# One PSUM bank tag: where the hash products stand while attention runs beside layer 1

## The chip, the core and the metric

The program runs on one core of one Trainium2 chip. TensorE (PE) multiplies into PSUM, which holds eight banks of 2 KB on each of 128 partitions; VectorE (DVE), ScalarE (ACT) and GpSimd (POOL) do the rest, and SyncE (SP) issues most DMAs. Each engine works through its own instructions in order and waits on semaphores for the others. The metric is the time of one execution in microseconds of device time; lower is better.

## What is computed

Two batches of eight heads of hashed attention feed two gated layers. Cut to what matters:

```python
q_bits = (einsum('bhsd,dk->bhsk', q, proj) > 0)      # 6 hash bits of each query, k_bits alike
mask   = q_bucket[:, :, :, None] == k_bucket[:, :, None, :]
scores = where(mask, scale * q @ k.T, -1e9)
attn   = softmax(scores);  x = attn @ v               # x: 1536 tokens x 512
g      = x @ w_gate                                   # layer 1, d_ff 1536
x      = (g * sigmoid(g) * (x @ w_val)) @ w_out
h      = x @ w_in                                     # layer 2, d_ff 2048
out    = (max(h, 0) + alpha * min(h, 0)) @ w_out2
```

## The kernel before

**Stages.** Tokens go in three chunks of 512. First the attention of chunk 0 runs alone. Then layer 1 of chunk 0 and of chunk 1 (`stage1`) run with the attention of the next chunk woven between their matrix products, two steps of attention to each step of layer 1 at most (`RATES`); this is the stretch "beside layer 1". After it come layer 1 of chunk 2 and layer 2 of all chunks, without attention.

**Attention.** An item is one pair of heads and 256 queries; it has two units, one for each head. A unit passes four parts, each a slot later than the one before (`LAGS`): `banks` (three score tiles `S` of two products each, copied out by ACT into `se`, their maxima `m` formed by DVE), `top` (the maxima transposed on PE into `mt`, reduced by DVE into `mq`), `back` (`mq` spread by PE into `mb`, subtracted by DVE at L341, exponent on ACT) and `values` (products with V into `po`, normalised by DVE as `xf` at L380).

**Hash products.** Preparing an item takes the hash of its queries, and each new pair of heads takes the hash of its keys in two pieces. `hash_mm` (L200 to L208) multiplies into a tile `hp` on PE; `hash_bits` (L212) reads it on DVE into the bits `mk`, and with that the bank is free; `hash_rows` (L218) copies `mk` into the operands of the scores on ACT. `mk` has one buffer. Beside layer 1 there are 21 such products: 8 for keys, all in the first third, and 13 for queries.

**Banks.** All PSUM tiles come from one pool, by tag: `at.nb` gives S three banks, T one, G two, Y one, po one. A tile of a tag must wait until the readers of the tile that last stood in its bank are done. Beside layer 1 the score tiles and `hp` take turns in the three banks of S, `mt` stands in Y, `mb` in T, the products of layer 1 (`gp`) in the two banks of G, and `po` in its own. The table is a line of its own:

```python
at.nb = dict(S=3, T=1, G=2, Y=1, po=1)
at.tag = dict(mt="G", mb="G", hp="T", po=("Y", "po"), gates="G")     # attention alone
at.tag = dict(mt="Y", mb="T", hp="S", po=("po", "po"), gates="G")    # beside layer 1
```

**Order.** The program text gives the order of the steps, and a scheduler then sets each engine's order from it, from the waits between the tiles and its own estimate of times; a few instructions are pinned. Weights come in as 64-bit words by DMA (`raw`, two buffers shared with the keys), are rounded by ACT (L596), DVE (L597, L599) and POOL (L601) into `wt`, split by ACT (L636) and DVE or POOL (L643) into `wb`, and the halves go to `gp` on PE at L699 to L701.

Of the kernel before, what the change touches and what calls it, by code (L numbers as in the profile page):

```python
# [54 lines left out]
def lsh_attention_moe_kernel(  # L55
# [13 lines left out]
    B, H, D, S = qT.shape  # L69
# [65 lines left out]
    at = Bag()  # L135
# [487 lines left out]
    def w_early():  # L623

        for w in early:
            r = raw_load(w)
            yield
            t = wp.tile([P, 512], F32, tag="wt", name="wt", bufs=WB[0])
            round64(r, t.bitcast(I32))
            yield  # L630
            nc.sync.dma_start(out=whole[w - F2I], in_=t)
            yield
# [231 lines left out]
        k += 1  # L864
        prime(k)
    at.alone = False
    at.tag = dict(mt="Y", mb="T", hp="S", po=("po", "po"), gates="G")
    early_steps = w_early()
    ws.pin = False
    ws.busy = True  # L870
# [98 lines left out]
```

## Time and profile before

| | |
|---|---|
| median of 3 runs | 845.91 us (845.59 to 846.26) |
| the profiled execution | 843.88 us |
| its span, first to last instruction | 842.0 us |
| beside layer 1 | about 118 to 445 us of the span |
| PE busy | 813.0 us, 97% |
| DVE, ACT, POOL busy | 536.6, 442.7, 347.5 us |

Three views are read. The windows give each engine's busy time and PE's granted clock in a stretch. The waits name who waited for whom. The timeline lists instructions: start, duration, engine, line, operation, what it writes and reads, and in square brackets the idle time of the engine just before it and what ended that. A product of PE overlaps the next one, so the distance between two starts (0.23 us for `gp`, 0.12 us for S) says more than a duration.

### The profile page before, as it was taken

To read this page: it belongs to the slowest core of one execution; us is meant where nothing else is said; L and a number is where in the kernel's file an instruction comes from. 1 tells how busy PE (TensorE), PEld (TensorE's weight loads), DVE (VectorE), ACT (ScalarE), POOL (GpSimd) and SP (SyncE) were. 2 spreads that over 40 slices of the span, in tenths; PEclk is the share of its full clock that TensorE was granted. 3 is DMA by queue.
4 is the path that set the end of the run, shared out by engine and by line. 5 is a ranking of instruction groups with operands and counts; after the bars stand their busy time and mean duration, and the time that the engine had idled before them with its cause. 6 is when DMAs were issued, how large, how long until landed. Compare 5 with 4: busy or idle time off the path is not lost.

```text
span 842.0 us, 11156 instructions
## 1 busy us (share of the span) xinstructions
PE 813.0 (97%) x3988; PEld 681.7 (81%) x3988; DVE 536.6 (64%) x826; ACT 442.7 (53%) x738; POOL 347.5 (41%) x284
## 2 busy tenths in 40 slices
PE   5998899998999999999999999999999999999998
PEld 4777778887888888888888888887888888888886
DVE  5889998887898866656675342348986533334332
ACT  7889877877766645555544232224433333333331
POOL 5133337666755633222221352333543354445441
PEclk9999999999999999999999999999999999999999
DMA  9223346867656547554554787784300300010001
GB/s 246 69 69 98 128 120 203 253 220 241 219 202 234 174 152 260 199 179 149 175 188 141 249 286 235 262 282 170 138 1 0 151 1 0 1 51 1 0 1 51
DMA packets 57287, 122.03 MB, mean 145 GB/s; under 512 B 16912, under 2 KB 29200, under 8 KB 56720
## 3 DMA queue, kind: packets, MB, share of 16 engines
q1 hardware_dynamic: 56080, 118.51, 42.3%
q0 software_dynamic: 1008, 2.75, 1.6%
q8 instruction: 32, 0.52, 0.3%
q14 instruction: 23, 0.19, 0.1%
q10 hardware_dynamic: 144, 0.05, 0.0%
HBM read 94.03 MB, written 27.26 MB: 144 GB/s over the span
## 4 chain that ended last, share of the span: by engine, by line
PE 70%; DVE 9%; DMA 7%; ACT 7%; issue 4%; POOL 1%; SPq 0%; DVEq 0%; ACTq 0%; POOLq 0%
PE po L358 9%; PE gp L699 8%; PE gp L701 8%; PE gp L700 8%; PE op L705 5%; PE op L706 5%; PE op L704 5%; DMA raw<-in_wblk_dram 5%; PE hp L700 5%; PE hp L699 5%; PE hp L701 5%; PE S L304 2%; PE S L305 2%; ACT se L306 2%; DVE wt L599 1%
## 5 line engine op out<-in xcount | busy, mean ns | idle before, releaser
L694 POOL TENSOR_TENSOR gl<-ex,gh 128x512 fp32r<-128x512 f32 x81 | 110.2, 1360 | 191.8 <-ACT gh L691 174.5
L358 PE MATMUL po<-se,vv 128*128 128x256 f32 x576 | 139.2, 381 | 5.4 <-ACT se L347 2.8
L691 ACT ACTIVATE gh<-ex 128x512 fp32r<-128x512 f32 x84 | 53.0, 631 | 137.1 <-DVE ex L688 86.6
L358 PEld LDWEIGHTS po<-se,vv 128*128 128x128 f32 x576 | 106.2, 190 | 22.7 <-ACT se L347 4.6
L699 PE MATMUL gp<-xh,wb 128*128 128x512 f32 x288 | 120.1, 417 | 0.5 <-ACT xh L383 0.5
L701 PE MATMUL gp<-xh,wb 128*128 128x512 f32 x288 | 112.9, 392 | 0.0
L700 PE MATMUL gp<-xl,wb 128*128 128x512 f32 x288 | 112.7, 391 | 0.0
L636 ACT ACTIVATE wb<-w 128x512 fp32r<-128x512 f32 x96 | 59.7, 628 | 71.4 <-PE hp L701 57.6
L601 POOL TENSOR_TENSOR wt<-wt,wr 128x512 int32<-128x512 int32 x48 | 63.4, 1327 | 81.1 <-DVE wt L599 32.8
L685 DVE TENSOR_SCALAR ex<-hp,al 128x512 f32<-128x512 f32 x48 | 35.9, 748 | 93.2 <-PE hp L701 92.0
L306 ACT ACTIVATE se<-S 128x512 f32<-128x512 f32 x144 | 81.9, 593 | 23.7 <-PE S L305 22.7
L304 PE MATMUL S<-QA,kt 128*128 128x256 f32 x288 | 79.6, 303 | 6.8 <-ACT se L306 3.0
L341 DVE SCALAR_TENSOR_TENSOR se<-se,mb 128x1536 f32<-128x1536 f32 x48 | 83.5, 1740 | 3.4 <-PE mb L336 3.4
L347 ACT ACTIVATE se<-se 128x1536 f32<-128x1536 f32 x48 | 71.1, 1482 | 8.8 <-DVE se L341 8.6
L705 PE MATMUL op<-wb,gh 128*128 128x512 f32 x192 | 74.8, 390 | 0.9 <-DVE wb L643 0.9
L305 PE MATMUL S<-qb,kt 76*128 76x256 f32 x288 | 73.9, 286 | 1.0 <-ACT kt L218 0.6
L706 PE MATMUL op<-wb,gl 128*128 128x512 f32 x192 | 74.7, 389 | 0.0
L699 PE MATMUL hp<-xh,wb 128*128 128x512 f32 x192 | 74.7, 389 | 0.0
L700 PE MATMUL hp<-xl,wb 128*128 128x512 f32 x192 | 74.7, 389 | 0.0
L701 PE MATMUL hp<-xh,wb 128*128 128x512 f32 x192 | 74.7, 389 | 0.0
L704 PE MATMUL op<-wb,gh 128*128 128x512 f32 x192 | 74.7, 389 | 0.0
L643 DVE TENSOR_TENSOR wb<-w,wb 128x512 fp32r<-128x512 f32 x65 | 56.1, 866 | 17.4 <-ACT wb L636 17.4
(99 smaller groups left out, 1666.7 us busy)
## 6 DMA issues: line engine op xcount, KB each, us to landing
wb<-w SPq DMA_DIRECT2D x72, 512.0 KB, 4.1
raw<-in_wblk_dram SPq DMA_DIRECT2D x68, 512.0 KB, 4.6
w<-wb SPq DMA_DIRECT2D x36, 512.0 KB, 3.0
qr<-in_q_dram SPq DMA_DIRECT2D x24, 256.0 KB, 2.9
nat<-in_k_dram SPq DMA_DIRECT2D x8, 384.0 KB, 3.4
vv<-in_v_dram SPq DMA_DIRECT2D x16, 192.0 KB, 5.6
whole<-wt SPq DMA_DIRECT2D x12, 256.0 KB, 2.2
w<-whole SPq DMA_DIRECT2D x12, 256.0 KB, 4.3
```

The lines of the kernel that those rows point to most:

```text
L304: nc.tensor.matmul(pt[:, i, :], lhsT=ka[:, sl], rhs=qa, start=True, stop=False)
L305: nc.tensor.matmul(pt[:, i, :], lhsT=kb[:, sl], rhs=qb, start=False, stop=True)
L306: nc.scalar.activation(out=u.se[:, 2 * j:2 * j + 2, :], in_=pt, func=AF.Copy)
L341: ins = nc.vector.scalar_tensor_tensor(out=u.se, in0=u.se, scalar=FLOOR, in1=u.mx[:, None, :].to_broadcast([P, NC, GQ]), op0=ALU.max, op1= ...
L358: nc.tensor.matmul(it.po[:, u.x, :], lhsT=VV[it.b, it.p][:, kb, u.x * D:u.x * D + P], rhs=u.se[:, kb, :], start=kb == 0, stop=kb == NC - 1)
L694: eng.tensor_tensor(out=l, in0=ex, in1=f32(h), op=ALU.subtract)
L699: nc.tensor.matmul(pt, lhsT=h, rhs=ah, start=first, stop=False)
L700: nc.tensor.matmul(pt, lhsT=h, rhs=al_, start=False, stop=False)
L701: nc.tensor.matmul(pt, lhsT=l, rhs=ah, start=False, stop=last)
L704: nc.tensor.matmul(pt, lhsT=gh, rhs=h, start=first, stop=False)
L705: nc.tensor.matmul(pt, lhsT=gh, rhs=l, start=False, stop=False)
L706: nc.tensor.matmul(pt, lhsT=gl, rhs=h, start=False, stop=last)
```

## The change

One tag: beside layer 1 `hp` now asks for the bank of tag Y, in which only `mt` stood, and no longer for one of the three of tag S. Sizes, counts and arithmetic stay.

```diff
-    at.tag = dict(mt="Y", mb="T", hp="S", po=("po", "po"), gates="G")
+    at.tag = dict(mt="Y", mb="T", hp="Y", po=("po", "po"), gates="G")
```

With other banks the scheduler finds other waits and sets some instructions elsewhere. In the rows below a name ends in the number of its tile, so that the two orders can be told apart; `waits` names the engines whose semaphores the instruction waits on.

PE, around the second piece of the keys' hash of the second new pair (hp_1808) and the next transposes; the order is the same on both sides, and the waits are not:

```order
 L206 MATMUL hp_1808<-kt1_125,skh_62 44x384
 L207 MATMUL hp_1808<-kt1_125,skl_63 44x384
-L304 MATMUL S_1813<-QA_1347,kt3_127 128x256 [waits Activation_49]
+L304 MATMUL S_1813<-QA_1347,kt3_127 128x256
 L305 MATMUL S_1813<-qb1_67,kt3_127 128x256
 L304 MATMUL S_1813<-QA_1347,kt3_127 128x256
...
 L330 MATMUL mt_1843<-ident_71,m2_1692 128x128 [waits DVE_49]
...
-L358 MATMUL po_1875<-se_1410,vv_386 128x256 [waits DVE_49,Activation_49]
+L358 MATMUL po_1875<-se_1410,vv_386 128x256 [waits PE_49,Activation_49]
 L358 MATMUL po_1875<-se_1410,vv_386 128x256
```

The score tile behind hp_1808 waits for nobody now; mt_1843 still waits on DVE, in the changed kernel for the reader of hp_1808 as well; and the po behind it no longer needs a wait on DVE of its own.

PE, around the second piece of the keys' hash of the third new pair (hp_2077), whose transposes are mt_2083:

```order
 L206 MATMUL hp_2077<-kt2_126,skh_62 44x384
 L207 MATMUL hp_2077<-kt2_126,skl_63 44x384
-L330 MATMUL mt_2083<-ident_71,m2_1957 128x128 x2
 L699 MATMUL gp_2062<-gh_1622,wb_1990 128x512
 L700 MATMUL gp_2062<-gl_1623,wb_1990 128x512
...
 L699 MATMUL gp_2062<-gh_1733,wb_1990 128x512
 L700 MATMUL gp_2062<-gl_1734,wb_1990 128x512
+L330 MATMUL mt_2083<-ident_71,m2_1957 128x128 x2
 L701 MATMUL gp_2062<-gh_1733,wb_1990 128x512
 L336 MATMUL mb_2100<-ident_71,mq_1963 128x128 x2
```

The transposes now stand behind five products of layer 1. Behind four of the hashes of queries the transposes move behind three products in the same way.

ACT, a little later, where the weights raw_2236 are rounded:

```order
 L596 ACTIVATE wr<-raw_2170 128x512
-L676 ACTIVATE ex<-gp 128x512
-L306 ACTIVATE se<-S 128x512
-L347 ACTIVATE se<-se 128x1536
-L306 ACTIVATE se<-S 128x512
-L636 ACTIVATE wb<-wt 128x512
-L306 ACTIVATE se<-S 128x512
-L218 ACTIVATE qb_66<-mk 12x256 x2
 L596 ACTIVATE wr<-raw_2236 128x512
```

The rounding of raw_2236 stands ahead of a tanh, three copies of scores and an exponent now, and no longer behind them; on DVE L597 and L599 for raw_2236 likewise stand ahead of a bit test L212, and SP issues that load two places earlier.

## Rows read from the trace of the kernel before

**Rows 1.** The page, part 1: busy time, share of the span, instructions.

```profile
PE 813.0 (97%) x3988; PEld 681.7 (81%) x3988; DVE 536.6 (64%) x826; ACT 442.7 (53%) x738; POOL 347.5 (41%) x284
```

**Rows 2.** Windows: stretch, length, busy PE, PEld, DVE, ACT, POOL, granted clock, DMA.

```profile
118.00:445.00 327.00, 321.55 (x1666) 273.72 (x1665) 249.15 (x400) 207.93 (x351) 151.35 (x119) 0.99 0.60 200
```

**Rows 3.** Waits of PE, 118 to 445 us: who for whom, total, times, longest.

```profile
PE po L358 <- DVE xf L380: 2.2, 3, 0.9
PE S L304 <- DVE mk L212: 1.7, 2, 1.4
PE hp L206 <- ACT se L306: 0.9, 1, 0.9
```

**Rows 4.** Timeline, PE and DVE, the first hash of keys beside layer 1.

```profile
136.76 0.53 PE L206 MATMUL hp<-kt,skh 128*44 128x384 f32 x1
...
137.38 0.41 DVE L331 TENSOR_REDUCE mq<-mt 128x2 f32<-128x256 f32 x1
```

**Rows 5.** Timeline, PE, a score tile that waits for a bit test.

```profile
155.56 0.28 PE L305 MATMUL S<-qb,kt 76*128 76x256 f32 x1
156.16 0.38 PE L304 MATMUL S<-QA,kt 128*128 128x256 f32 x1 [0.32 <-DVE mk L212]
```

**Rows 6.** Timeline, PE, the transposes mt_1843 and the po behind them.

```profile
169.55 0.38 PE L330 MATMUL mt<-ident,m 128*128 128x128 f32 x2
...
172.06 1.10 PE L358 MATMUL po<-se,vv 128*128 128x256 f32 x4 [0.53 <-DVE xf L380]
```

**Rows 7.** Timeline, DVE, the same time, and a later L179 for comparison.

```profile
165.68 2.49 DVE L179 TENSOR_TENSOR kt<-nat,kt 64x768 fp32r<-64x768 f32 x1
168.20 1.68 DVE L599 SCALAR_TENSOR_TENSOR wt<-raw,wt 128x512 int32<-128x512 int32 x1
172.55 0.60 DVE L212 TENSOR_SCALAR mk<-hp,ck 44x384 f32<-44x384 f32 x1
...
193.09 0.95 DVE L179 TENSOR_TENSOR kt<-nat,kt 64x768 fp32r<-64x768 f32 x1
```

**Rows 8.** Windows, as rows 2: before and during the low clock.

```profile
190.00:194.00 4.00, 1.90 (x9) 1.13 (x8) 3.90 (x7) 1.47 (x3) 2.74 (x4) 1.00 0.96 204
194.73:198.20 3.47, 3.47 (x13) 2.66 (x11) 1.54 (x4) 3.39 (x7) 1.76 (x3) 0.52 0.92 336
```

**Rows 9.** Timeline, PE, the stretch with the longest waits.

```profile
192.53 0.38 PE L304 MATMUL S<-QA,kt 128*128 128x256 f32 x1 [1.37 <-DVE mk L212]
...
194.98 0.63 PE L330 MATMUL mt<-ident,m 128*128 128x128 f32 x2
...
198.33 1.03 PE L358 MATMUL po<-se,vv 128*128 128x256 f32 x4
```

**Rows 10.** Timeline, PE and DVE, what leads to the two bit tests there.

```profile
182.39 0.38 PE L336 MATMUL mb<-ident,mq 128*128 128x128 f32 x2
...
183.96 0.43 DVE L597 TENSOR_SCALAR wt<-raw 128x512 int32<-128x512 int32 x1 [3.70 <-DMA raw<-in_wblk_dram]
...
185.84 1.74 DVE L341 SCALAR_TENSOR_TENSOR se<-se,mb 128x1536 f32<-128x1536 f32 x1
...
191.90 0.57 DVE L212 TENSOR_SCALAR mk<-hp,ck 44x384 f32<-44x384 f32 x1
...
196.87 0.61 DVE L212 TENSOR_SCALAR mk<-hp,ck 44x384 f32<-44x384 f32 x1 [1.93 <-ACT kt L218]
```

**Rows 11.** Timeline, SP and ACT, the load of raw_2236 and its rounding.

```profile
203.65 2.42 SPq L579 DMA_DIRECT2D raw<-in_wblk_dram  x2
...
209.09 0.68 ACT L596 ACTIVATE wr<-raw 128x512 int32<-128x512 uint32 x1 [0.34 <-DMA raw<-in_wblk_dram]
```

**Rows 12.** Timeline, PE and DVE, a later hash of queries and the po behind it.

```profile
274.08 0.38 PE L330 MATMUL mt<-ident,m 128*128 128x128 f32 x2
...
274.52 0.47 DVE L212 TENSOR_SCALAR mk<-hp,cq 44x256 f32<-44x256 f32 x1
...
286.98 1.10 PE L358 MATMUL po<-se,vv 128*128 128x256 f32 x4 [0.91 <-DVE xf L380]
```

## The prediction

> **What bounds the kernel now.** I read the page first, then the stretch that the change touches, then PE's waits in it. PE is busy for 813.0 of 842.0 us [rows 1]: every other engine counts only where PE waits for it. Beside layer 1, from 118 to 445 us, PE is busy for 321.55 of 327 us [rows 2], so all waits there come to 5.5 us, 0.65% of the kernel. That is the frame for a gain. The waits name three causes [rows 3]: `po` waits for the normalisation `xf` (2.2 us, three times), a score tile waits for a bit test `mk` (1.7 us, twice), and a hash product waits for a copy of scores (0.9 us, once). The last two are what sharing the three banks of S costs: `hp` stands in one of them until DVE has read it, or waits until one is free. A fourth cost has no wait of its own: from 194.73 to 198.20 us the granted clock is 0.52, the lower of two levels (1.2 and 2.4 GHz), after PE had worked for only 1.90 of the 4 us from 190 to 194 [rows 8]; 3.47 us at 0.52 lose 1.7 us. So at most 1.7 + 0.9 + 1.7 = 4.3 us hang on the bank.
>
> **What the change removes and adds.** No instruction is added or removed, so the whole cost lies in waits. Gone are the waits of score tiles for `mk`. New are two on the bank of Y: a hash product must wait until `mq` has read the last `mt` there, and the next `mt` until `mk` has read the hash product. PE stands in order behind either. I go through the 21 hash products with the times of the trace and keep a ledger of how late PE is against the trace of before; DVE's times are kept until something pushes them.
>
> *At 137 us.* The hash product starts at 136.76 and `mq` ends at 137.38 + 0.41 = 137.79 [rows 4]. Restarting takes 0.06 us more (`mk` ends at 192.47, the score tile behind it starts at 192.53 [rows 9, 10]). The scheduler fills some 0.4 us of the 1.1 us with one product of layer 1. PE is **0.7 us late**.
>
> *At 156 us.* The score tile that starts 0.60 us after its forerunner, where 0.12 us is usual, no longer waits; with the slower restart that is 0.6 us back [rows 5]. Late: **0.1 us**.
>
> *At 169 us, the main term.* `mt` starts at 169.55 [rows 6]. The hash product before it is read at 172.55 to 173.15, because DVE is held by a 2.49 us L179 and a 1.68 us L599 [rows 7]. DVE's order there is not changed. So PE stands from about 169.6 to 173.2, 3.6 us, and is 3.7 us late at the transposes. The 0.53 us that `po` waited for `xf`, and the slower restart behind that wait, are swallowed [rows 6]: 0.6 us back. Late: **3.1 us**. Bounds: 1.5 us less if L179 takes the 0.95 us that it takes at 193.09 [rows 7]; nothing more, as nothing else is queued there.
>
> The Trainium skill (Perfetto Trace Analysis, section Matmuls) says that independent groups of products should rotate through different PSUM banks, so that the reading of one overlaps the next. By it this wait belongs to the change as such and the three banks were the better place, which speaks for the second rival below; this row agrees with the rule, the score tile at 156 us speaks against it.
>
> *The clock behind it.* PE does nothing for 3.6 us here; before, 1.90 us of work in 4 us were followed by the low level [rows 8]. I take it that the low level follows here too and costs the same 1.7 us. Late: **4.8 us**. Bounds: 0 and 1.7.
>
> *From 182 to 199 us: most of it is given back.* PE's own waits at 190 to 194 us and its low clock there came from DVE being late, and a late PE meets them with its time already lost. DVE sets the end. It waits for a DMA until 183.96, then L341 starts at 185.84, the first bit test at 191.90, and the second, which waits for ACT to copy the bits out of the one `mk` buffer, at 196.87 [rows 10]. If PE is 4.8 us late, `mb` comes at 187.2 instead of 182.39 and ends near 187.5, so L341 is pushed by 1.7 us, and all of DVE behind it. The second bit test then ends at 196.87 + 0.61 + 1.7 = 199.2. `mt_2083` now waits for it; the five products that moved ahead of it are done by then. With the transposes (0.14 us), one product (0.3) and `mb` (0.2) behind it, `po` starts near 199.9 instead of 198.33 [rows 9]. Late: **1.6 us**. Without the low clock `mb` would end at 185.9, L341 would hardly be pushed, and PE would be level with before: bounds 0 and 1.6, and 4.8 if nothing is given back.
>
> *From 203 to 210 us.* The rounding of raw_2236 stands ahead of a tanh and three score copies on ACT, and ahead of a bit test on DVE. Its load took 5.4 us from issue to use (203.65 to 209.09) [rows 11]; it is issued earlier now, behind fewer stores, but ACT and DVE get there earlier as well, and the test's transposes wait behind all that. Nothing in the trace shows ACT waiting there; between 0 (landed in time) and 2 us (part of the 5.4 us uncovered). I take 0.5, nearer to nothing because the load moves ahead with its reader. Late: **2.1 us**.
>
> *From 243 us on.* The remaining waits of `po` for `xf`, 2.2 - 0.5 - 0.9 = 0.8 us near 243 and 0.91 us at 286.98 [rows 3, 12], let PE catch up, since `xf` comes from DVE: 1.3 us are left after the first. At 274.08 `mt` meets a bit test that ends at 274.52 + 0.47 = 274.99 [rows 12]: 1.0 us more, 2.3. The second `xf` takes back 0.9: 1.4. Where the scheduler moved the transposes behind three products (four times), the products take about the time that the bit test needs; other score tiles that need no wait now give back a little: 0.1 us less in all. Behind 300 us PE does not wait beside layer 1, so what is late then stays late: **1.3 us**.
>
> **The sum.** 0.7 - 0.6 + 3.6 - 0.6 + 1.7 - 3.2 + 0.5 - 0.8 + 1.0 - 0.9 - 0.1 = 1.3 us. The profiled span becomes 843.3, with the 1.9 us around it 845.2; the runs' median lies 2.0 us above the profiled execution, so 845.9 + 1.3 = **847.2 us**. A measurement of this kernel tells about 0.2%, 1.7 us, from no change.
>
> **Rivals.**
> *No low clock, all given back.* The wait at 169 us is as above but the clock stays. Then the ledger reads 0 at 198 us, 0.5 at 210, 0 after the first `xf`, 1.0 at 275 and 0.1 after the second: 846.0 us. For it: PE has worked almost without a gap before 169 us; against it: the 3.6 us without work are longer than any wait of rows 3.
> *Slower: the delay is passed on.* DVE waits 3.70 us for a load before 183.96 [rows 10]. I took that as fixed. If the load moves too, since its buffer and the DMA queue wait for ACT and DVE work that waits for PE, then L341, both bit tests and the next transposes all move by up to 4.8 us and nothing in 182 to 199 us gives it back. With a push of 3.5 us instead of 1.7 the end is 3.3 us late: 849.2 us. It decides from a push of about 2.1 us on. Against it: the rounding of weights does not read PSUM.
> *Faster: the freed bank pays.* If the DVE chain at 184 to 197 us comes some 2 us earlier, by an earlier load or shorter DVE work at 165 to 170 us, `mt_2083` can start at 195.5, the score tile and the hash product of rows 9 and 3 go at once, and the low clock never comes: 2 us before the old time, 843.9 us. For it: the waits of rows 3 are surely gone; against it: the bit test at 196.87 depends on DVE and ACT, not on the bank.
> The Trainium skill (SBUF — State Buffer, section Who interferes with whom) says that a DVE instruction with two SBUF inputs contends with a GpSimd instruction that reads SBUF. L179 is such a one, and its 2.49 against 0.95 us agrees with that; by it the long time would come again, which speaks against this rival.
> *The change does nothing* is out: the scores' waits are gone from the order, and `hp` and `mt` now wait for each other.
>
> **How the numbers follow.** Forecast 0.48, no low clock 0.17, passed on 0.24, faster 0.11. The range runs from between the last rival and the old time to a little above the third case: 844.8 to 849.6 us; it leaves out most of the faster case and the worst of the slower one. Slower by over 0.2% (above 847.6): the passed-on case and a sixth of the forecast, 0.32. Faster: 0.11. Within: 0.57.
>
> **What would show it.** In the changed trace: a wait of PE at an `mt` for `mk` of 3 to 4 us near 170 us (if none, the main term is wrong); a low clock near 174 us and none near 195; the second bit test between 197 and 200 us and the transposes right behind it; the waits of `po` for `xf` smaller than 2.2 us; a wait of 1 us at an `mt` near 275. If PE's waits beside layer 1 come to less than 4 us in all, the faster case holds; if DVE's L341 near 186 us starts after 188, the slower one.

## The result and the profile after

The changed kernel takes 851.21 us in the median of 6 runs (849.81 to 854.37), the kernel before 845.61 us beside it: a ratio of 1.0073 (95% interval 1.0054 to 1.0092). It is slower by 5.6 us, where 1.3 us were forecast and 849.6 was the upper end. Measured a second time (the run `again` below) the ratio was 1.0058 (1.0036 to 1.0079). The profiled execution took 850.75 us, 6.9 us more than that of before, with a span of 848.9 us.

Part 1 of the page after, which answers to [rows 1]:

```profile
PE 815.3 (96%) x3988; PEld 681.7 (80%) x3988; DVE 541.4 (64%) x826; ACT 443.0 (52%) x738; POOL 343.5 (40%) x284
```

PE's waits from 118 to 450 us (who for whom, total, times, longest), for [rows 3]:

```profile
PE mt L330 <- DVE mk L212: 6.2, 4, 4.1
PE hp L206 <- DVE mq L331: 0.9, 1, 0.9
PE gp L699 <- ACT xh L383: 0.6, 1, 0.6
PE po L358 <- DVE xf L380: 0.6, 1, 0.6
PE hp L206 <- issue: 0.4, 1, 0.4
```

No score tile waits for a bit test any more, as the change says. In its place the transposes wait for bit tests, 6.2 us in four places. The timeline of PE gives the places, for [rows 6, 9, 12]:

```profile
173.92 0.44 PE L330 MATMUL mt<-ident,m 128*128 128x128 f32 x2 [4.08 <-DVE mk L212]
...
199.76 0.44 PE L330 MATMUL mt<-ident,m 128*128 128x128 f32 x2 [1.02 <-DVE mk L212]
...
221.88 0.44 PE L330 MATMUL mt<-ident,m 128*128 128x128 f32 x2 [0.35 <-DVE mk L212]
...
225.70 0.34 PE L206 MATMUL hp<-kt,skh 128*44 128x384 f32 x1 [0.87 <-DVE mq L331]
...
278.20 0.44 PE L330 MATMUL mt<-ident,m 128*128 128x128 f32 x2 [0.71 <-DVE mk L212]
...
290.81 1.10 PE L358 MATMUL po<-se,vv 128*128 128x256 f32 x4 [0.56 <-DVE xf L380]
```

DVE, for [rows 7, 10]:

```profile
166.39 2.50 DVE L179 TENSOR_TENSOR kt<-nat,kt 64x768 fp32r<-64x768 f32 x1
...
173.26 0.60 DVE L212 TENSOR_SCALAR mk<-hp,ck 44x384 f32<-44x384 f32 x1
...
184.86 0.43 DVE L597 TENSOR_SCALAR wt<-raw 128x512 int32<-128x512 int32 x1 [0.50 <-DMA raw<-in_wblk_dram]
186.53 0.69 DVE L312 TENSOR_TENSOR m<-S,se 128x512 f32<-128x512 f32 x1 [1.24 <-PE mt L330]
...
188.07 1.75 DVE L341 SCALAR_TENSOR_TENSOR se<-se,mb 128x1536 f32<-128x1536 f32 x1
...
199.09 0.61 DVE L212 TENSOR_SCALAR mk<-hp,ck 44x384 f32<-44x384 f32 x1 [1.92 <-ACT kt L218]
```

Windows (stretch, length, busy PE, PEld, DVE, ACT, POOL, granted clock, DMA), for [rows 8]:

```profile
169.90:173.90 4.00, 0.00 (x0) 0.00 (x0) 3.75 (x8) 1.52 (x4) 3.04 (x5) 1.00 0.80 245
174.00:178.00 4.00, 4.00 (x13) 3.27 (x14) 3.54 (x5) 2.49 (x6) 2.56 (x2) 0.57 0.68 187
194.70:198.20 3.50, 3.50 (x21) 2.94 (x20) 2.37 (x6) 3.44 (x6) 3.24 (x3) 1.00 1.03 268
594.30:597.70 3.40, 3.40 (x9) 2.63 (x9) 3.40 (x5) 2.57 (x5) 2.19 (x2) 0.51 0.02 5
```

PE stands still for 4.0 us, and then works at 0.57 of its full clock, near the lower level of 1.2 GHz. Near 195 us, where before had its low clock, there is none. A second low clock has come at the start of layer 2.

The ledger of PE's lateness is read by counting: the n-th product of layer 1 (`gp`), from 586 us on the n-th `op` of layer 2, is the same product in every kernel, and each row gives how many us later it starts than in the first profile of before, whose time names the row. "Again" is a second profile of the changed kernel, "before again" a second one of before (both runs below).

| at (us of before) | forecast | after | again | before again |
|---|---|---|---|---|
| 144 | 0.7 | 0.7 | 1.0 | 1.0 |
| 162 | 0.1 | 0.1 | 2.9 | 2.8 |
| 179 | 4.8 | 5.2 | 7.8 | 2.0 |
| 187 | - | 5.3 | 7.8 | 7.9 |
| 196 | - | 1.8 | 4.3 | 4.7 |
| 199 | 1.6 | 2.2 | 5.7 | 3.6 |
| 212 | 2.1 | 2.3 | 5.8 | 3.6 |
| 237 | 2.1 | 4.0 | 7.2 | 5.0 |
| 245 | 1.3 | 3.2 | 6.5 | 5.5 |
| 278 | 2.3 | 4.2 | 7.8 | 5.4 |
| 446 | 1.3 | 4.1 | 8.4 | 4.8 |
| 598 | 1.3 | 6.9 | 11.0 | 5.2 |

Up to 212 us the first profile after follows the forecast within 0.6 us. It leaves it between 212 and 237 us, and once more between 586 and 598 us. The agreement up to 212 us is with that one execution: at 162 us, where the forecast has 0.1, the second profile of the changed kernel stands at 2.9 and that of before at 2.8. Two profiles of one kernel differ by as much as the two kernels do.

### The profile page after: what moved, and what is told of

It is laid out like the page before. It is cut to its first block, busy times and chain, and to the rows that moved or that the text cites. A ratio compares the mean times of both kernels' runs of the same rounds, so it can differ in the third digit from the quotient of the medians.

```text
span 848.9 us, 11158 instructions
## 1 busy us (share of the span) xinstructions
PE 815.3 (96%) x3988; PEld 681.7 (80%) x3988; DVE 541.4 (64%) x826; ACT 443.0 (52%) x738; POOL 343.5 (40%) x284
## 4 chain that ended last, share of the span: by engine, by line
PE 69%; DVE 10%; ACT 9%; DMA 6%; issue 3%; POOL 2%; SPq 0%; DVEq 0%; ACTq 0%; POOLq 0%
PE po L358 9%; PE gp L699 8%; PE gp L701 8%; PE gp L700 8%; PE op L705 5%; PE op L706 5%; PE op L704 5%; PE hp L700 5%; PE hp L699 5%; PE hp L701 5%; DMA raw<-in_wblk_dram 3%; ACT se L306 2%; PE S L304 2%; PE S L305 2%; ACT se L347 2%
## 5 line engine op out<-in xcount | busy, mean ns | idle before, releaser
L694 POOL TENSOR_TENSOR gl<-ex,gh 128x512 fp32r<-128x512 f32 x81 | 108.7, 1342 | 198.4 <-ACT gh L691 181.9
L341 DVE SCALAR_TENSOR_TENSOR se<-se,mb 128x1536 f32<-128x1536 f32 x48 | 83.6, 1742 | 3.4 <-PE mb L336 3.4
L705 PE MATMUL op<-wb,gh 128*128 128x512 f32 x192 | 75.3, 392 | 2.2 <-DVE wb L643 2.2
L643 DVE TENSOR_TENSOR wb<-w,wb 128x512 fp32r<-128x512 f32 x65 | 56.2, 867 | 18.6 <-ACT wb L636 18.5
```

The source lines that it names most:

```text
L694: eng.tensor_tensor(out=l, in0=ex, in1=f32(h), op=ALU.subtract)
L705: nc.tensor.matmul(pt, lhsT=gh, rhs=l, start=False, stop=False)
```

## The experiments

All times are set against runs of before on the same chip; single runs of before ranged from 843.2 to 852.2 us on the later chips. "Late" is the ledger's number against the first profile of before; "step" is what is added between 586 and 598 us. The same kernel against itself, `before_again`, shows what a ratio is worth: 1.0011, with an interval of 0.2% to either side.

| kernel | hash products in the bank of `mt` | ratio (95%) | late at 237 | at 446 | step |
|---|---|---|---|---|---|
| again | all 21 | 1.0058 (1.0036-1.0079) | 7.2 | 8.4 | 2.6 |
| keys_in_Y | 8 of keys | 1.0043 (1.0026-1.0061) | 8.3 | 7.8 | 1.4 |
| queries_in_Y | 13 of queries | 0.9991 (0.9974-1.0008) | 0.9 | 1.3 | 0.7 |
| hash_in_T | none; all in that of `mb` | 1.0025 (1.0005-1.0045) | 1.1 | 1.7 | 2.8 |
| before_again | none | 1.0011 (0.9988-1.0034) | 5.0 | 4.8 | 0.3 |
| fill_wait | all | 1.0107 (1.0081-1.0133) | 6.6 | 7.2 | 2.9 |
| two_mk_Y | all, two bit buffers | 1.0040 (1.0022-1.0058) | 3.3 | 3.5 | 0.2 |
| two_mk_S | none, two bit buffers | 0.9995 (0.9979-1.0011) | -0.9 | -0.8 | 3.1 |
| piece2_in_S | all but 1 | 1.0042 (1.0021-1.0062) | 8.2 | 8.2 | 3.0 |
| piece3_in_S | all but 1 | 1.0037 (1.0020-1.0054) | 4.3 | 3.4 | 2.7 |
| piece4_in_S | all but 1 | 1.0064 (1.0039-1.0090) | 4.5 | 9.3 | 0.7 |
| pieces34_in_S | all but 2 | 1.0047 (1.0022-1.0072) | 6.8 | 8.1 | 1.5 |
| pieces23_in_S | all but 2 | 1.0027 (1.0005-1.0049) | 2.8 | 6.1 | 1.6 |
| pieces234_in_S | all but 3 | 1.0025 (1.0007-1.0044) | 2.5 | 3.2 | 2.9 |
| first_in_S | second pieces and queries | 1.0066 (1.0044-1.0089) | 5.0 | 6.0 | 0.3 |
| both_cures | queries, two bit buffers | 0.9983 (0.9970-0.9997) | 0.7 | 1.2 | 2.9 |

### The same kernels once more

> The changed kernel once more, unaltered. It tells a step that the change brings from one that only its first profiled execution had. Theory A (the waits in the bank of the transposes are the loss, and the step at the start of layer 2 is a load that landed late in that one execution): the wait near 174 us is 4.1 us again, PE is 4.0 us late from 235 to 583 us, and the step of 2.9 us near 588 to 598 us (a wait of 2.2 us at L705 and a low clock behind it) is gone or much smaller; median 849.5 to 851.5 us. Theory B (a PE that comes 4 us late meets its weights in another phase there, every time): the step is there again, 2.5 to 3 us, median 851 to 852 us.

> The kernel before once more, unaltered, for a second profile of it. The changed kernel came twice with a step of 2.6 to 2.9 us at the start of layer 2 against the first profile of before, and the variant with the hash products in T with 2.8 us, though PE's instructions there are the same. Theory A (the step hangs on when loads land, and every kernel has it in some of its executions): this profile shows a wait of about 2 us at L705 and a low clock behind it near 590 to 598 us as well, and differs from the first profile of before by 1 us or more at 300 us too, since the loads of weights land at other times. Theory B (it needs a PE that is late): no such step, within 1 us of the first profile all along.

PE in the second profile of the changed kernel:

```profile
154.71 0.28 PE L206 MATMUL hp<-QA,sqm 128*44 128x256 f32 x1 [0.69 <-DVE mq L331]
...
160.96 0.44 PE L330 MATMUL mt<-ident,m 128*128 128x128 f32 x2 [1.40 <-DVE mk L212]
...
176.39 0.44 PE L330 MATMUL mt<-ident,m 128*128 128x128 f32 x2 [3.79 <-DVE mk L212]
...
203.29 0.44 PE L330 MATMUL mt<-ident,m 128*128 128x128 f32 x2 [2.04 <-DVE mk L212]
```

PE in the second profile of before:

```profile
158.95 0.39 PE L304 MATMUL S<-QA,kt 128*128 128x256 f32 x1 [2.15 <-DVE mk L212]
...
185.31 0.58 PE L304 MATMUL S<-QA,kt 128*128 128x256 f32 x1 [2.84 <-ACT se L306]
...
222.47 0.39 PE L304 MATMUL S<-QA,kt 128*128 128x256 f32 x1 [1.54 <-ACT se L306]
```

Both theories of the first run fell in part: PE came 8.4 us late out of the attention instead of 4.0, though the wait near 174 us was the same 3.8 us, and the step at layer 2 was there again (2.6 us). The second profile of before has no such step (0.3 us), but it is 4.8 us late at 446 us as well; it waits for 2.15 us at a score tile where the changed kernel lost 0.69 + 1.40 us, and 2.84 us near 185 with a low clock behind (0.50 from 186 to 190 us). So a ledger from one profile of each kernel can say what a wait costs there, but its sum carries an uncertainty of some 4 us. The difference of the kernels has to be taken from the medians.

Four kernels tell where the step at the start of layer 2 comes from. ACT copies the first weights that come back from DRAM (`w<-whole`), DVE takes its part from that copy, PE waits at L705. Before, after, two_mk_S and first_in_S:

```profile
569.23 1.93 ACT L636 ACTIVATE wb<-w 128x512 fp32r<-128x512 f32 x3 [0.47 <-DMA w<-whole]
...
587.60 0.50 PE L705 MATMUL op<-wb,gh 128*128 128x512 f32 x1 [0.95 <-DVE wb L643]
```

```profile
574.59 1.93 ACT L636 ACTIVATE wb<-w 128x512 fp32r<-128x512 f32 x3 [1.78 <-DMA w<-whole]
...
592.87 0.50 PE L705 MATMUL op<-wb,gh 128*128 128x512 f32 x1 [2.17 <-DVE wb L643]
```

```profile
570.10 1.92 ACT L636 ACTIVATE wb<-w 128x512 fp32r<-128x512 f32 x3 [2.09 <-DMA w<-whole]
...
588.36 0.50 PE L705 MATMUL op<-wb,gh 128*128 128x512 f32 x1 [2.47 <-DVE wb L643]
```

```profile
575.64 1.97 ACT L636 ACTIVATE wb<-w 128x512 fp32r<-128x512 f32 x3 [0.85 <-DMA w<-whole]
...
593.91 0.50 PE L705 MATMUL op<-wb,gh 128*128 128x512 f32 x1 [1.21 <-DVE wb L643]
```

ACT comes to the load by the same instructions each time. In before, first_in_S, after and two_mk_S it uses the load 4.2, 4.6, 5.5 and 5.8 us after SP has issued it, and waits for it 0.47, 0.85, 1.78 and 2.09 us; PE then waits 0.95, 1.21, 2.17 and 2.47 us. The later the load lands, the longer PE waits. After the two long waits a low clock follows (0.51 in after, 0.54 in two_mk_S), after the two short ones none. two_mk_S has its hash products among the scores and has the step; first_in_S and two_mk_Y have the keys' second pieces in the bank of `mt` and hardly have it (0.3 and 0.2 us). The step belongs to the landing of a load in that execution, not to the change.

### Keys or queries, and another bank

The edits, cut to the lines that matter:

```diff
-            hash_mm(it, it.QA, it.QB[0:96], sqm, sq0, GQ)
+            hash_mm(it, it.QA, it.QB[0:96], sqm, sq0, GQ, at.tag["hq"])
-    at.tag = dict(mt="Y", mb="T", hp="Y", po=("po", "po"), gates="G")
+    at.tag = dict(mt="Y", mb="T", hp="Y", hq="S", ...)    # keys_in_Y
+    at.tag = dict(mt="Y", mb="T", hp="S", hq="Y", ...)    # queries_in_Y
+    at.tag = dict(mt="Y", mb="T", hp="T", ...)            # hash_in_T
```

> The 8 hash products of keys beside layer 1 in the bank of the transposes, the 13 of queries back among the three banks of scores. Theory A (the loss comes from the bit tests of keys, which stand behind long DVE work): PE is 3.5 to 4.5 us late at 235 us and stays so, median 849 to 851.5 us. Rival (the transposes that moved behind three or five products, and the bit tests of queries, are the loss): PE is at most 2 us late at 300 us, median 846 to 848 us.

> The converse: keys among the banks of scores, the 13 hash products of queries in the bank of the transposes. Theory A: nothing is late until 240 us, then the wait of 0.7 us near 275 us and the two waits for the normalised output smaller: within 0.5 us of the kernel before at 300 us, median 845 to 847 us. Rival (queries are the loss): 2 us or more late at 300 us, median 848 us or more.

> All 21 hash products in the bank of the broadcast maxima, which stands one part later and is read by the long subtraction on DVE. Theory A (whoever shares a single bank with a hash product stands behind the bit test on DVE, and the bit test is what is late): PE waits near 170 to 175 us for the bit test again, now at the broadcast instead of the transposes, 3.5 to 4.5 us, and the hash products wait for the subtraction as well; 4 to 8 us late at 300 us, median 849 to 854 us. Rival (it is the bank of the transposes that is the wrong one, because their reduction is short of time): no wait over 2 us there, median within 2 us of the kernel before, 844 to 848 us.

With the queries' products alone in the bank of `mt` nothing is lost that can be measured (0.9991); with the keys' alone most of the loss is there (1.0043). The ledgers were expected smaller: 3.5 to 4.5 us at 235 us for the keys, where 8.3 came, and 0.5 us at 300 us for the queries, where 1.1 came. And the 8.3 us of keys_in_Y are not all the doing of that bank: 5.4 of them arose from 150 to 162 us, where PE waited 4.03 us at a score tile for the bit test of a query, which stands among the scores there, with a low clock behind it.

PE's waits with the products in T:

```profile
PE mb L336 <- DVE mk L212: 7.3, 5, 2.3
PE hp L206 <- DVE se L341: 0.9, 2, 0.7
```

Theory A had 3.5 to 4.5 us for the longest wait there and 4 to 8 us of lateness; it is 2.3 and 1.7 us. In T too, a single bank, PE stands behind the bit test: at 173.22 us the broadcast waits until about the time at which the transposes start in after (173.92), but PE comes to it later and has less left to wait. The ratio, 1.0025, lies between the two kernels.

### The wait and its clock

```diff
-        for x in range(2):
+        for x in list(range(2)) * n:    # n = 5 for this one product, else 1
```

> The changed kernel with one hash product (second piece of the keys of the second new pair) computed five times over in its bank, 16 more products of 0.18 us that start from zero each time, so the bits are the same: PE has 2.9 us of work in the place where it waits for the bit test near 170 us. It parts the wait from the clock. Theory A (the wait is DVE's time, and the low clock behind it comes from PE's standing still): the wait near 174 us shrinks from 3.8-4.1 us to 0.8-1.4 us, no low clock follows, PE stands at the next transposes (near 184 us) about 1 us earlier than in the changed kernel's own profiles; median 0.5 to 1.5 us under the changed kernel, 850.5 to 852 us on this chip. Rival (the low clock comes for another reason): the low clock is still there, or the 2.9 us are added to the end.

```profile
176.35 0.44 PE L330 MATMUL mt<-ident,m 128*128 128x128 f32 x2 [1.15 <-DVE mk L212]
...
202.43 0.44 PE L330 MATMUL mt<-ident,m 128*128 128x128 f32 x2 [2.83 <-DVE mk L212]
```

```profile
176.40:180.40 4.00, 4.00 (x20) 3.42 (x21) 3.97 (x6) 3.44 (x7) 3.98 (x4) 1.00 0.49 140
```

With work in its place the wait shrinks from 4.08 to 1.15 us and the clock stays at 1.00. From 162 to 179 us PE loses 3.3 us, where after and again lost 5.1 and 4.9: the low clock costs 1.5 to 1.8 us there, the forecast's term. But the end is not earlier: the next transposes wait 2.83 us for the second bit test of the third pair. The expected gain of 0.5 to 1.5 us did not come; the whole is slower still (1.0107), and why is open. The edit is not clean: from 173 to 195 us it also sets some roundings, splits and key work of DVE, ACT and POOL in another order, which may have its part in the 2.83 us. The profile is no later at 446 us (7.2 us) than that of again (8.4).

### A second buffer of bits

```diff
-        mk = at.sm.tile([44, S // 2], F32, tag="mk", name="mk", bufs=1)[:, :w]
+        mk = at.sm.tile([44, S // 2], mybir.dt.bfloat16, tag="mk", name="mk", bufs=2)[:, :w]
```

> The changed kernel with two buffers of bits instead of one (in a 16-bit type, so that they take the same room; the bits are 0, 1 and -1, so nothing is lost): a bit test no longer waits for ScalarE to copy the bits of the one before it. Theory A (of the loss, the part near 200 us is the second bit test, which waits 1.9 us for that copy): the wait of the transposes near 200 us (1.0 and 2.0 us in two profiles) is gone, the one near 174 us stays at 3.8-4.1 us; median 1 to 2 us under the changed kernel. Rival (loads alone make the bit tests late): no change, within 0.5 us.

> The same second buffer of bits in the kernel before. Theory A: the hash product and score tiles near 192 to 197 us wait less; 0 to 1.5 us faster than the kernel before. Rival: no change.

```profile
197.33 0.61 DVE L212 TENSOR_SCALAR mk<-hp,ck 44x384 bf16<-44x384 f32 x1 [0.47 <-PE hp L207]
```

In two_mk_Y the second bit test no longer waits 1.92 us for ACT's copy, and the wait of the transposes near 200 us is gone; the next ones, at 210 us, wait 1.17 us instead. The ratio falls to 1.0040; from the changed kernel's 1.0058 to 1.0073 that is 1.5 to 2.8 us. The intervals overlap, so the size is not firm. In the kernel before the same buffer wins nothing that can be measured.

### Which pieces

```diff
-            lambda: box.append(hash_mm(it, a, a, skh, skl, w, tag)),
+            lambda: box.append(hash_mm(it, a, a, skh, skl, w, "S" if (it.b, it.p, i) in MOVED else tag)),
```

`MOVED` stands for the pieces that go back among the scores, which each run names in its own condition: the second piece of the second, third or fourth new pair (2, 3, 4), and for first_in_S every first piece.

> The changed kernel with one hash product back among the banks of scores: the second piece of the keys of the second new pair, whose bit test causes the longest wait (3.7 to 4.1 us near 174 us). No engine's order changes. Theory A (that wait is only moved: the kernel before stands still later, behind the same late work of DVE, near 185 to 197 us, and has its low clock there): the wait near 174 us is gone, a wait of 1.5 to 4 us and a low clock come near 185 to 203 us instead, PE is as late at 240 us as in the changed kernel to within 1.5 us; ratio to the kernel before 1.004 to 1.007. Rival (the longest wait is the loss): nothing comes in its place, 4 to 5 us less late at 240 us; ratio 0.999 to 1.002.

> The changed kernel with the second piece of the keys of the third new pair back among the banks of scores; its bit test stands behind the copy of the bits of the first piece, near 199 to 203 us. The transposes behind it go back to their old place on PE, and the rounding of one block of weights and its load too. Theory A (of the loss of 4.7 us, some 1.9 us arise here): the wait of 1 to 2.8 us at the transposes near 200 us is gone; ratio to the kernel before 1.003 to 1.005. Rival (the wait near 174 us is the loss): 1.0055 to 1.007 as in the changed kernel.

> The changed kernel with the second piece of the keys of the fourth new pair back among the banks of scores; it then stands ahead of the po products near 224 us again, and nothing else moves. Theory A (1.3 us arise here: the hash product waits 0.87 us for the reduction of the last transposes, and it splits a group of po products): from 212 to 237 us PE loses 0 to 0.7 us against the first profile of before instead of 1.3 to 1.9; ratio to the kernel before 1.003 to 1.006. Rival: the same 1.3 to 1.9 us, ratio as in the changed kernel.

> Both of the last two pieces back among the banks of scores; the wait near 174 us stays. Theory A: what is left of the loss is a wait that takes the place of one the kernel before has anyway: ratio to the kernel before 0.999 to 1.003, the wait near 174 us 3.5 to 4.5 us all the same. Rival (the wait near 174 us is the loss): ratio 1.004 to 1.007.

None of these pieces alone holds the loss: 1.0042, 1.0037, 1.0064 (expected 1.003 to 1.006), and 1.0047 for the last two, where theory A wanted 0.999 to 1.003 and fell. PE with the longest wait taken away (piece2_in_S):

```profile
189.80 1.13 PE L358 MATMUL po<-se,vv 128*128 128x256 f32 x4 [1.53 <-ACT se L347]
...
204.04 0.44 PE L330 MATMUL mt<-ident,m 128*128 128x128 f32 x2 [2.93 <-DVE mk L212]
```

The ledger there stands at 4.8 us at 162 and 5.1 us at 179, so nothing is lost near 174; but it goes from 4.2 us at 196 to 8.1 us at 204. In this profile the wait has moved to the next bit test, with a low clock behind it.

A query's product can cost as much. In piece4_in_S DVE waited 3.85 us for a load of weights and then took 1.64 us at an L643 (0.68 in before), and the transposes of the 278 us row waited 2.98 us for the bit test of a query; a low clock followed, and PE lost 4.7 us between the rows of 270 and 278 us:

```profile
272.86 0.43 DVE L597 TENSOR_SCALAR wt<-raw 128x512 int32<-128x512 int32 x1 [3.85 <-DMA raw<-in_wblk_dram]
```

```profile
282.61 0.69 PE L330 MATMUL mt<-ident,m 128*128 128x128 f32 x2 [2.98 <-DVE mk L212]
```

pieces23_in_S shows the same (3.78 and 2.88 us, 4.6 us lost). In the other profiles with this product in the bank of `mt` the wait is 0.59 to 1.15 us. In before, with the product among the scores, PE passes the place without a wait at 274.08, though the bit test ends only at 274.99 [rows 12].

The four runs below take several pieces at once.

> The changed kernel with the second pieces of the keys of the second, third and fourth new pair back among the banks of scores; the first pieces and the queries stay in the bank of the transposes. Theory C (the three waits stand in for one another: PE stands at the next transposes for whatever DVE is late, so it takes all three): 3 us or more of the loss go, ratio to the kernel before 1.000 to 1.0025, no wait of transposes over 1.5 us between 165 and 235 us. Rival D (the first pieces have a part, and the queries once DVE is late): 1.003 to 1.006.

> The converse for the keys: all four first pieces back among the banks of scores, the four second pieces stay in the bank of the transposes. Theory C: the loss stays, 1.0045 to 1.007, with waits of 3 to 4 us near 174 us and 1 to 3 us near 200 us. Rival D: 1.000 to 1.003.

> The changed kernel with the second pieces of the second and third new pair back among the banks of scores. Theory C: between the single pieces and all three, 1.001 to 1.0035. Rival D: 1.0035 to 1.006.

> Keys among the banks of scores, queries in the bank of the transposes, and two buffers of bits in a 16-bit type. Each alone came out level with the kernel before (0.9991 and 0.9995). If each wins some half a microsecond: 0.997 to 0.9995. If they win nothing: 0.9995 to 1.001.

Theory C fits: 1.0027 with two, 1.0025 with three pieces back, the latter at the edge of what it gave, and 1.0066 with all first pieces back, which help nothing. The intervals of the first two reach into what rival D gave. What stays open is the rest of pieces234_in_S, 0.0025 or some 2 us (0.6 to 3.7). The queries alone do not show it (0.9991), and no run has the first pieces alone in the bank. Its waits show the kernel before's place of the loss near 194 us, where a key's product waits for a bank of scores (0.92 us in before):

```profile
PE hp L206 <- ACT se L306: 3.7, 1, 3.7
```

both_cures (0.9983, 0.9970 to 0.9997) is the only kernel whose whole interval lies below 1, by 1.4 us in the middle. That is less than the 0.2% that a measurement can tell.

## Why the prediction was wrong

*What held.* PE as the bound; the score tiles' waits for `mk` and the hash product's wait for ACT [rows 3] that go; the wait near 170 us (3.6 forecast, 4.08, 3.79 and, in the other kernels with this piece in the bank, 3.7 to 4.1, but 0.8 in keys_in_Y, which had lost 4.0 us just before); the low clock behind it, 1.7 forecast and 1.5 to 1.8 measured; none near 195; the second bit test at 199.09 with the transposes 0.67 us later; the `po` waits down from 2.2 to 0.6 us (1.3 in again); the wait near 275 us (1.0 forecast, 0.71 and 1.07, but 2.98 and 2.88 in two later kernels). The giving back between 182 and 199 us, the boldest step, is there: 3.2 us forecast, 3.1 in after and 2.1 in again, which had given back 3.4 by 196 us and lost some again at the second bit test. The load of raw_2236 (0.5 forecast) cost PE 0.1 us from 199 to 212 us, though ACT stood 3.67 us for it at 208.03.

The marker of the slower rival was met: L341 started at 188.07, a push of 2.2 us, and the rival was to decide from about 2.1 on. Its mechanism was not what pushed. The load came 0.9 us later (184.86 for 183.96), but after it DVE waited 1.24 us for PE's transposes, as the forecast had it with a late PE, and PE was 2.2 us late behind the second bit test, not 3.3. (By the forecast's own terms a push of 3.5 us ends at 1.3 + 1.8 = 3.1 us, 849.0 and not 849.2.)

*First failed step: from 212 to 237 us the ledger has no term.* I passed from 210 to 243 us. There the last key product (hp_2341) now asks for the bank of `mt`, must wait for the reduction of the transposes, and the scheduler sets it behind the first `po` product and not ahead of `mb`. PE, after the change (-) and with this piece back among the scores (+):

```
+L206 MATMUL hp_2341<-kt3_127,skh_62 44x384
 L336 MATMUL mb_2346<-ident_71,mq_2212 128x128 x2
...
-L358 MATMUL po_2372<-se_1911,vv_1604 128x256
-L206 MATMUL hp_2341<-kt3_127,skh_62 44x384
...
-L358 MATMUL po_2372<-se_1911,vv_1604 128x256 x3
+L358 MATMUL po_2372<-se_1911,vv_1604 128x256 x4
```

It waits 0.87 us at 225.70, the transposes before it 0.35 and the `po` 0.23: 1.45 us, and the ledger gains 1.7 us in after, 1.4 in again, 1.7 in first_in_S; with the piece put back 0.4, 0.9 and -0.2 in piece4_in_S, pieces34_in_S and pieces234_in_S. Over all profiles the gain is 0.1 to 2.9 us with this piece in the bank of `mt` (nine profiles, mean 1.5) and -0.4 to 1.4 with it among the scores (seven, mean 0.5). The 1.4 is before_again, which waited 1.54 us there for ACT: the term is right in the mean, and a single profile does not show it. The order of the instructions showed the move; I had not costed it. In the first profile this term and the second `xf` (0.4 us given back, not 0.9) make 2.2 of the 2.8 us that separate it from the forecast at 446 us.

*Second failed step: "what is late stays late" and the span.* The profiled sum ended at 446 us; 2.9 us came at 586 to 598 us from a late load. Not the change's doing, but a cost that single executions have or don't have: 0 to 3.1 us in the kernels with all keys among the scores, 0.2 to 3.0 in the others.

*Third failed step: the waits of one execution.* The median that I added to was right (845.9 for 845.6). But I took the waits from one execution, and 843.88 us was among the fastest that before has (843.2 to 852.2). Executions differ in when weights land (near 270 us DVE waits for a load not at all in after and 3.85 us in piece4_in_S), and with that in when DVE reaches its bit tests. In the three banks of scores a late bit test stops PE only when PE needs that bank again, behind the tiles of the other two; in the one bank of `mt` it stops PE at the very next transposes. It does stop PE among the scores as well: 2.15 us in before_again, 2.76 in queries_in_Y, 4.03 in keys_in_Y. My reading is that the change therefore costs more in a mean execution than in the one I worked from.

Three profiles with the keys among the scores and one bit buffer (before, before again, queries_in_Y) stand at 0, 4.8 and 1.3 us at 446 us, mean 2.0; four with the second pieces in the bank of `mt` (after, again, keys_in_Y, first_in_S) at 4.1, 8.4, 7.8 and 6.0, mean 6.6. The difference, 4.5 us, is close to the medians' 4.7 to 5.6 (4.1 without keys_in_Y, much of whose lateness arose among the scores). Seven profiles are few for a spread of 4 us, so the means support this cause and don't prove it. Nor are slow executions all of it: the lowest run of again (849.24) lies 4.8 us above the lowest of before beside it (844.47). What is shown is that the keys alone bring most of the loss and that none of their second pieces alone holds it; that a wait taken away comes back at the next bit test is shown in one profile. How the 4.7 to 5.6 us divide between the second bit tests, the moved product and the loads is open.

*L179.* I bounded the main term by 1.5 us less if L179 took 0.95 instead of 2.49 us. The second profile of the changed kernel had just that:

```profile
171.38 0.95 DVE L179 TENSOR_TENSOR kt<-nat,kt 64x768 fp32r<-64x768 f32 x1
...
175.73 0.60 DVE L212 TENSOR_SCALAR mk<-hp,ck 44x384 f32<-44x384 f32 x1
```

The wait was 3.79 us all the same, since DVE came to L179 later. The Trainium skill's rule (SBUF — State Buffer, section Who interferes with whom), that a DVE instruction with two SBUF inputs contends with a GpSimd instruction that reads SBUF, agrees with these two: POOL worked at L179 and L694 from 166.22 to 170.04 us beside the long one in after, and stood still beside the short one in again. Which of the two is held up is not always DVE: beside the 0.95 us at 193.09 [rows 7] POOL's own L179 started 0.05 us later and took 2.60 us.

## What to carry to other kernels

A bank that stands free for most of the time is not a free bank: a tile put there ties the next user on PE to the queue of the engine that reads the tile, and three rotating banks absorb more of a late reader than one does. When an order changes, cost every place where it does, and not those alone that stand near the waits of the old profile. And take a second profile of the same kernel before a sum of less than its spread is believed: here two of one kernel differed by 4.8 us.

## What the runs showed of the hardware

The same DMA, four loads of weights issued together, was waited for by ACT for 0.47 to 2.09 us in four executions, with the same instructions ahead of it; PE's loss at L705 followed with some 0.4 us on top, and after the long waits a low clock of about 3.4 us (0.51 to 0.54) added another 1.7 us. With a 4 us wait of PE filled by repeated products the clock stayed at 1.00, and nothing was won at the end: PE waited 2.83 us for DVE at the next transposes.
